# Moving three steps' query and key transposes from TensorE to the crossbar DMA in an attention-and-mixer kernel

## The chip, the core and the metric

The kernel runs on one core of a Trainium2 chip. The core has a matrix engine (TensorE; PE in the profile, with its weight loads as PEld), a vector engine (VectorE, DVE), a scalar engine (ScalarE, ACT), GpSimd (POOL), a queue processor that only issues work (SyncE, SP), and 16 DMA engines. Each engine runs its own list of instructions in order and waits on semaphores for the others. The metric is the device time of one execution in microseconds, lower being better; the number compared is the median of several executions.

## What is computed

An attention layer with squared ReLU in place of softmax feeds an MLP mixer. Sizes: batch 8, 12 heads, sequence 448, head size 64, so a model width of 768.

```python
scores = (q @ k.T) / sqrt(64)                   # per batch and head, 448 x 448
attn   = maximum(scores, 0)**2 / 448
x      = (attn @ v), heads side by side         # 8 x 448 x 768
u      = x + (maximum(x.T @ w_tok1, 0) @ w_tok2).T     # token mixing, 448 -> 256 -> 448
out    = u + maximum(u @ w_ch1, 0) @ w_ch2             # channel mixing, 768 -> 1536 -> 768
```

Matrix products take bf16 operands; inputs and output are float32.

## The kernel before, in words

**Steps.** The work is cut into 24 steps of four heads each (`ND`, three steps to a batch element). For step i the kernel needs queries and keys with the head dimension on the partitions, so the loaded tiles `q_raw` and `k_raw`, which have tokens on the partitions, must be transposed. Then seven score tiles (`scores`, L211) go through ScalarE's ReLU (L231) and VectorE's squaring (L238); `values` (L240) multiplies them with v into the two PSUM tiles `acc0` and `acc1`; `values_out` (L259) scales the result into `xT`.

**Mixer.** One step behind, `x_back` transposes `xT` back to tokens (by TensorE up to step 7, by DMA from step 8 on: `XDMA` = 8, L294), `token1`, `token1_main` and `token1_rest` (L339, L355) and `token2` (L380, L390) do the token mixing and write `uT_sb`. Units of channel mixing, `channel1` (L431) and `channel2` (L470, output addition L477), are put in a Python list, and `fill` hands them out between the pieces of the steps by a credit in nominal cost, so that TensorE always has something to do. The order of instructions is fixed when the program is built; nothing is reordered at run time.

**The residual.** The addition at L477 needs u with tokens on the partitions. `u_back` (L407) gets it by DMA transposes of `uT_sb` into `u_sb` (L413), two transfers per step of heads, issued on SP. Six of them, those of batch element 0, are issued at the end of loop pass i = 7, and `hold_back` (L418) makes them wait: GpSimd writes one element into each target after it has read `uT_sb` of that pass, so no transfer may start sooner. A second `hold_back`, in pass 8, stands ahead of the next six.

**Transposing q and k.** Up to step 11 `transposes` (L125) does it on TensorE: 56 small products into `acc0` and `acc1` (L140), then two copies by VectorE (L154). From step 12 on (`TDMA` = 12) VectorE first interleaves the two tiles into `qk_sb` (`interleave`, L192, one buffer), and one DMA transpose, issued on SP, writes `qkT_x` (`transposes_dma`, L198). `qk_of` (L204) picks the layout by the same constant. The DMA form is prepared two passes ahead, the TensorE form one pass ahead.

**Queues.** SP issues, in program order, all DMA transposes (L198, L294, L413) and the output transfers (L489). GpSimd issues the loads of q, k and v three steps ahead (`load_four`, L83), and of the weights. `out_sb` has three buffers, `raw` tiles have four of each name, and the two PSUM tiles tagged `bank` serve all channel products in turn.

The loop from L661 on is where the order is written out by hand. Pass i holds, in this order: two score tiles of step i, the values of step i-1, a third score tile, interleaving and fill, `x_back`, the residual's transfers, `transposes_dma`, the loads, squares, two score tiles, TensorE transposes of step i+1, squares, fill, first token product, two score tiles, squares, fill, second token product, `hold_back` and the six residual transfers (pass 7 only), squares, fill.

Of the kernel before, what the change touches and what calls it, by code (L numbers as in the profile page):

```python
# [16 lines left out]
def kernel(  # L17
# [19 lines left out]
    ND = B * H // 4  # L37
# [143 lines left out]
            else:  # L181
                nc.vector.tensor_copy(sb[:, :, 0], queries[:, :, :S])

    TDMA = 12
    qk_tiles = {}

    def interleave(i):

        t = attn.tile([128, 2, QC, 2, D], BF16, name="qk_sb", bufs=1)
        qk_tiles[i] = t  # L190
        for w in range(2):
            nc.vector.tensor_copy(  # L192
                t[:, w].rearrange("n c g d -> n g c d"), raws.pop((i, "qk"[w]))
            )

    def transposes_dma(i):
        sb = attn.tile([128, 2, QC, 128], BF16, tag="qkT", name="qkT_x", bufs=3)
        nc.sync.dma_start_transpose(  # L198
            out=sb.rearrange("n w c t -> n (w c) t"),
            in_=qk_tiles.pop(i).rearrange("n w c g d -> n (w c g d)"),  # L200
        )
        qkT[i] = sb

    def qk_of(i, h, r):  # L204
        sb = qkT[i]
        if i < TDMA:
            return sb[h, r, 0, :], [sb[h, r, 1, c * 64 : (c + 1) * 64] for c in range(QC)]
# [3 lines left out]
    def scores(i, c, alone=False):  # L211
        ps = ps_att.tile([128, 2, 512], FP32, tag="att", name="sc_ps")
        for r in range(2):
            for g in range(2):
                h = slice(64 * g, 64 * (g + 1))
                queries, keys = qk_of(i, h, r)
                nc.tensor.matmul(  # L217
                    ps[64 * r : 64 * (r + 1), g, :S],
                    lhsT=keys[c],
                    rhs=queries,  # L220
                    start=True,
                    stop=True,
                    skip_group_check=True,
                )
        at = attn.tile([128, 2, S], BF16, name="at", bufs=11)
        if alone:
            nc.vector.tensor_scalar(
                out=at, in0=ps[:, :, :S], scalar1=0.0, scalar2=None, op0=ALU.max
            )
        else:  # L230
            nc.scalar.activation(at, ps[:, :, :S], AF.Relu)  # L231
        squares.append(at)
        at2[i, c] = at

    def square(keep=0):
        while len(squares) > keep:
            at = squares.pop(0)
            nc.vector.tensor_tensor(out=at, in0=at, in1=at, op=ALU.mult)  # L238

    def values(i, cs):  # L240
        v_raw = raws[i, "v"]
        if i not in accs:
            accs[i] = [ps_acc.tile([128, 512], FP32, tag=f"acc{r}", name="acc_ps") for r in range(2)]
        ps = accs[i]
        for c in cs:
            at = at2.pop((i, c))
            for r in range(2):
                for g in range(2):
                    h = slice(64 * r, 64 * (r + 1))
                    nc.tensor.matmul(  # L250
                        ps[r][64 * g : 64 * (g + 1), :S],
                        lhsT=v_raw[h, g, c, :],
                        rhs=at[h, g, :],
                        start=(c == 0),
                        stop=(c == QC - 1),
                        skip_group_check=True,
                    )

    def values_out(i, split=False):  # L259
        b, d = divmod(i, DB)  # L260
        ps = accs.pop(i)
        for r in range(2):
            if split and r == 1:
                nc.scalar.activation(
                    xT[b % 2][:, 2 * d + r, :S], ps[r][:, :S], AF.Copy, scale=float(alpha2)
                )
                continue
            nc.vector.tensor_scalar(  # L268
                out=xT[b % 2][:, 2 * d + r, :S],
                in0=ps[r][:, :S],  # L270
                scalar1=float(alpha2),
                scalar2=None,
                op0=ALU.mult,
            )
        if i > 2 * DB - 1:
            for r in range(2):
                nc.vector.tensor_scalar(
                    out=xT[b % 2][:, 2 * d + r, S:],
                    in0=ps[r][:, S - 64 : S],
                    scalar1=float(alpha2),  # L280
                    scalar2=None,
                    op0=ALU.mult,
                )
# [119 lines left out]
    def chunks(b):  # L403
        half = NT // 2
        return range(half) if b % 2 == 0 else range(half, NT)
# [12 lines left out]
    def hold_back(b, src):  # L418

        u_tiles[b] = mix.tile([128, NP, NT - NT // 2, 128], BF16, name="u_sb", bufs=3)  # L420
        for p in range(NP):
            nc.gpsimd.tensor_copy(u_tiles[b][:1, p, 0, :1], src)

    def channel1(b, e):
        if b % 2 == 0 and e == 0 and b > 0:
            r2_tiles[b // 2] = mix.tile([128, EC, 2 * S], BF16, name="r2_sb")
        uT, r2 = uT_tiles[b // 2], r2_tiles[b // 2]
        off = (b % 2) * S
        ps = ps_mm.tile([128, 512], FP32, tag="bank", name="m1_ps")
        for g in range(CC):  # L430
            nc.tensor.matmul(  # L431
                ps[:, :S],
                lhsT=wc1[:, g, e * 128 : (e + 1) * 128],
                rhs=uT[:, g, off : off + S],
                start=(g == 0),
                stop=(g == CC - 1),
            )
        nc.scalar.activation(r2[:, e, off : off + S], ps[:, :S], AF.Relu)  # L438
# [87 lines left out]
    def channel_work(b):  # L526
        for e in range(2 if b == 0 else 0, EC):
            queue.append((C1, lambda e=e: channel1(b, e)))
        for t in chunks(b):
            for j in range(2):  # L530
                last = b == B - 1 and t == NT - 1 and j == 1
                unit = channel2_last if last else channel2
                args = (b, t) if last else (b, t, j)
                later.append((C2, lambda unit=unit, args=args: unit(*args)))
        if b > 0:
            queue.extend(later)
            later.clear()
# [91 lines left out]
    i = DB  # L629
# [31 lines left out]
    for i in range(DB + 1, ND + 2):  # L661
        slow = i <= 2 * DB
        back = i - 1 < ND
        if i == 2 * DB + 1:
            rate[0] = (EC * C1 + NT * C2) / DB
        if i < ND:
            scores(i, 0)
            scores(i, 1)
        if 0 <= i - 1 < ND:
            values(i - 1, range(QC))  # L670
            values_out(i - 1)
        if i < ND:
            scores(i, 2)
        if TDMA <= i + 2 < ND:
            interleave(i + 2)
        if i - 1 < XDMA:
            fill(1 / 3, least=1)
        if 0 <= i - 1 < ND:
            x_back(i - 1)
        since[0] = 0.0  # L680
        if i > 2 * DB + 1:
            if i == 2 * DB + 2:
                hold_back(1, x_tiles[i - 1][:1, 0, 0, :1])
            while u_later and u_later[0] < max(i - 1 - (i == 2 * DB + 2), 0):
                u_back(u_later.pop(0))
        if TDMA <= i + 2 < ND:
            transposes_dma(i + 2)
        if i + PRE < ND:
            if i - 1 >= XDMA:
                nc.gpsimd.tensor_copy(gate, x_tiles[i - 1][:1, 1, 3, 127:])  # L690
            load_four(i + PRE)
        if i == 5:
            load_wc2(1, 2)
            load_wt1_last()
        square()
        if i - 1 >= XDMA:
            fill(0.37, least=1)
        if i < ND:
            scores(i, 3)
            scores(i, 4)  # L700
        if i + 1 < min(ND, TDMA):
            transposes(i + 1)
        square()
        if slow:
            token1(i - 1)
            fill(1 / 3, least=1)
        else:
            fill(0.37, least=1, upto=4400 if back else 0)
            if back:
                token1_main(i - 1)  # L710
        if i < ND:
            if not slow:
                token1_rest(i - 1)
            scores(i, 5)
            scores(i, 6)
        elif back:
            token1_rest(i - 1)
        if not slow:
            square()
            fill(0.1, least=1)  # L720
        if back:
            token2(i - 1)
            if (i - 1) % DB == DB - 1:
                channel_work((i - 1) // DB)
        if i == 2 * DB + 1:
            hold_back(0, uT_tiles[1][:1, 0, :1])
            for _ in range(DB):
                u_back(u_later.pop(0))
        square()
        fill(1 / 3 if slow else 0.16, least=1)  # L730
    while queue:
        queue.pop(0)[1]()
# [30 lines left out]
```

## Time and profile before

| what | value |
|---|---|
| median of 10 runs | 371.26 us (370.96 to 373.02) |
| the profiled execution | 371.23 us |
| its span in the profile | 369.5 us |
| TensorE busy | 359.9 us, 97% of the span |
| VectorE / ScalarE / GpSimd busy | 207.3 / 210.3 / 98.4 us |
| DMA moved | 48.75 MB, mean 132 GB/s |
| TensorE clock granted | 0.999 |

The span begins with the first and ends with the last recorded instruction; the execution's own time is 1.7 us longer. A matrix engine that is busy 97% of the time is the first place to look, but a share is only an average: the view of the chain of work that ended last tells stage by stage whether it waited for anything. Loop pass 7 begins at about 69.5 us of the span, pass 8 at 84.4, pass 9 at 101.7, pass 10 at 116.8, pass 11 at 131.9.

### The profile page before, as it was taken

The numbers are of one execution on the slowest core, as the hardware profiler recorded it, in microseconds if no ns is written. First come the engines' busy times: TensorE is split into PE (matmuls) and PEld (weight loads), VectorE is DVE, ScalarE is ACT, GpSimd is POOL, SyncE is SP. The second block draws the span as 40 slices with busy tenths as digits, with TensorE's granted clock in tenths as the row PEclk, the third lists the DMA queues.
The fourth block names the chain that finished last, engine by engine and source line by source line (L and its number), as shares of the span: only waits on it lengthen the run. The fifth ranks groups of instructions, "written<-read, shape, count | busy, mean of one in ns | idle before, by whom it ended". The sixth has DMA issues, their size and how long they took to land.

```text
span 369.5 us, 8951 instructions
## 1 busy us (share of the span) xinstructions
PE 359.9 (97%) x3705; PEld 193.8 (52%) x3705; DVE 207.3 (56%) x414; ACT 210.3 (57%) x313; POOL 98.4 (27%) x185
## 2 busy tenths in 40 slices
PE   8889999999999999999999999999999999999995
PEld 3534555455555544555455545455445555555563
DVE  2986688756675774565654674575564674221031
ACT  3987888777245467735775457753875456402400
POOL 8957348112312404430421403412300000000000
PEclk9999999999999999999999999999999999999999
DMA  8999999952999899869768889859682624233023
GB/s 152 123 192 189 185 207 133 169 76 57 128 180 159 131 239 141 157 118 209 138 110 152 127 184 181 142 100 208 127 145 52 135 56 89 59 71 87 0 70 103
DMA packets 91449, 48.75 MB, mean 132 GB/s; under 512 B 65360, under 2 KB 87952, under 8 KB 91408
## 3 DMA queue, kind: packets, MB, share of 16 engines
q0 software_dynamic: 24496, 21.49, 41.5%
q1 hardware_dynamic: 66528, 26.26, 33.5%
q8 instruction: 29, 0.48, 0.5%
q10 hardware_dynamic: 384, 0.43, 0.4%
q14 instruction: 12, 0.10, 0.1%
HBM read 43.42 MB, written 11.01 MB: 147 GB/s over the span
## 4 chain that ended last, share of the span: by engine, by line
PE 88%; DVE 7%; ACT 1%; DMA 1%; issue 1%; POOL 0%; DVEq 0%; POOLq 0%; ACTq 0%
PE m_ps L470 29%; PE m_ps L431 28%; PE acc_ps L250 9%; PE sc_ps L217 9%; PE h_ps L380 4%; PE t_ps L339 3%; DVE at L238 3%; PE t_ps L321 1%; DVE uT_sb L390 1%; DMA q_raw<-in_q_dram 1%; PE t_ps L355 1%; ACT at L231 1%; PE qkT_ps L140 1%; DVE qkT L154 1%; PE x_ps L303 1%
## 5 line engine op out<-in xcount | busy, mean ns | idle before, releaser
L231 ACT ACTIVATE at<-sc_ps 128x896 bf16<-128x896 f32 x167 | 144.7, 924 | 49.4 <-PE sc_ps L217 45.0
L238 DVE TENSOR_TENSOR at<-at 128x896 bf16<-128x896 bf16 x168 | 98.1, 620 | 61.8 <-ACT at L231 61.7
L431 PE MATMUL m_ps<-uT_sb,wc 128*128 128x448 bf16 x564 | 115.7, 353 | 0.4 <-DVE out_sb L477 0.2
L470 PE MATMUL m_ps<-wc,r_sb 128*128 128x384 bf16 x660 | 113.2, 326 | 0.0
L470 PEld LDWEIGHTS <-r_sb 128*128 128x128 bf16 x660 | 62.7, 98 | 47.9 <-issue 7.5
L438 ACT ACTIVATE r_sb<-m_ps 128x448 bf16<-128x448 f32 x94 | 51.5, 548 | 53.4 <-PE m_ps L431 53.4
L431 PEld LDWEIGHTS <-wc 128*128 128x128 bf16 x564 | 52.3, 98 | 56.3 <-issue 11.6
L477 DVE TENSOR_TENSOR out_sb<-m_ps,u_sb 128x384 f32<-128x384 f32 x55 | 30.5, 554 | 46.8 <-PE m_ps L470 46.8
L250 PE MATMUL acc_ps<-at,v_raw 64*64 64x448 bf16 x672 | 40.7, 351 | 1.5 <-DVE x_sb L312 0.7
L268 DVE TENSOR_SCALAR xT<-acc_ps 128x448 bf16<-128x448 f32 x45 | 26.1, 619 | 27.6 <-PE acc_ps L250 27.6
L83 POOL DMA_DIRECT2D q_raw<-in_q_dram x48 | 29.0, 614 | 23.7 <-DMA wc<-in_moe_w_ch_dram 20.2
L690 POOL COPY gate<-x_sb 1x1 bf16<-1x1 bf16 x12 | 2.3, 192 | 122.3 <-DMA x_sb<-xT 122.3
L390 DVE TENSOR_TENSOR uT_sb<-h_ps,xT 128x448 bf16<-128x448 f32 x48 | 27.7, 616 | 9.4 <-PE h_ps L380 9.3
L83 POOL DMA_DIRECT2D v_raw<-in_v_dram x48 | 29.6, 643 | 6.9 <-DMA wc<-in_moe_w_ch_dram 5.5
L250 PEld LDWEIGHTS <-v_raw 64*64 64x64 bf16 x672 | 21.4, 106 | 15.7 <-issue 5.7
L365 ACT ACTIVATE r_sb<-t_ps 128x256 bf16<-128x256 f32 x36 | 11.9, 381 | 30.2 <-PE t_ps L355 30.2
L217 PE MATMUL sc_ps<-qkT 64*64 64x448 bf16 x336 | 27.5, 360 | 1.1 <-ACT at L231 1.0
L83 POOL DMA_DIRECT2D k_raw<-in_k_dram x46 | 28.1, 634 | 1.8 <-issue 1.7
L217 PE MATMUL sc_ps<-qkT_x 64*64 64x448 bf16 x336 | 25.7, 356 | 0.0
L380 PE MATMUL h_ps<-wt,r_sb 128*128 128x448 bf16 x96 | 22.3, 353 | 0.0
L217 PEld LDWEIGHTS <-qkT 64*64 64x64 bf16 x336 | 9.2, 105 | 13.0 <-issue 10.8
L339 PE MATMUL t_ps<-x_sb,wt 128*128 128x256 bf16 x108 | 14.7, 273 | 0.0
(62 smaller groups left out, 162.9 us busy)
## 6 DMA issues: line engine op xcount, KB each, us to landing
out_dram<-out_sb SPq DMA_DIRECT2D x54, 192.0 KB, 3.1
q_raw<-in_q_dram POOLq DMA_DIRECT2D x48, 112.0 KB, 4.6
v_raw<-in_v_dram POOLq DMA_DIRECT2D x48, 112.0 KB, 6.0
k_raw<-in_k_dram POOLq DMA_DIRECT2D x46, 112.0 KB, 6.1
wc<-in_moe_w_ch_dram POOLq DMA_DIRECT2D x4, 1152.0 KB, 12.5
u_sb<-uT_sb SPq DMA_TRANSPOSE x48, 2.5
x_sb<-xT SPq DMA_TRANSPOSE x16, 3.2
k_first<-in_k_dram SPq DMA_DIRECT2D x1, 224.0 KB, 3.5
```

The source lines that it names most:

```text
L83: eng.dma_start(out=dst[64 * r : 64 * (r + 1)].rearrange("p g c d -> p g (c d)"), in_=src[b, h0 : h0 + 2].rearrange("g (p c) d -> p g (c d ...
L217: nc.tensor.matmul(ps[64 * r : 64 * (r + 1), g, :S], lhsT=keys[c], rhs=queries, start=True, stop=True, skip_group_check=True,)
L231: nc.scalar.activation(at, ps[:, :, :S], AF.Relu)
L238: nc.vector.tensor_tensor(out=at, in0=at, in1=at, op=ALU.mult)
L250: nc.tensor.matmul(ps[r][64 * g : 64 * (g + 1), :S], lhsT=v_raw[h, g, c, :], rhs=at[h, g, :], start=(c == 0), stop=(c == QC - 1), skip_gro ...
L268: nc.vector.tensor_scalar(out=xT[b % 2][:, 2 * d + r, :S], in0=ps[r][:, :S], scalar1=float(alpha2), scalar2=None, op0=ALU.mult,)
L380: nc.tensor.matmul(parts[r][:, :S], lhsT=r1[:, j, r * 128 : (r + 1) * 128], rhs=wt2[:, j, :], start=(j == 0), stop=(j == JC - 1),)
L390: nc.vector.tensor_tensor(out=uT_tiles[b // 2][:, 2 * d + r, off : off + S].rearrange("n (c p) -> n c p", c=QC), in0=parts[r][:, :S].rearr ...
L431: nc.tensor.matmul(ps[:, :S], lhsT=wc1[:, g, e * 128 : (e + 1) * 128], rhs=uT[:, g, off : off + S], start=(g == 0), stop=(g == CC - 1),)
L438: nc.scalar.activation(r2[:, e, off : off + S], ps[:, :S], AF.Relu)
L470: nc.tensor.matmul(ps[:, :HN], lhsT=r2[:, e, t * 128 : (t + 1) * 128], rhs=wc2[:, e, cols], start=(e == 0), stop=(e == EC - 1),)
L477: nc.vector.tensor_tensor(out=o[:, cols].rearrange("n (g d) -> n g d", d=128), in0=ps[:, :HN].rearrange("n (g d) -> n g d", d=128), in1=u_ ...
```

## The change

`TDMA` goes from 12 to 9, so queries and keys of steps 9, 10 and 11 go by the crossbar too. Steps 9 and 11 are prepared at the loop's usual place, in passes 7 and 9. Step 10 would have been prepared in pass 8; it is prepared at the end of pass 7 instead, ahead of `hold_back` and the six residual transfers on the program's list. The last `square()` of a pass moves above these lines.

```diff
-    TDMA = 12
+    TDMA = 9
...
-        if TDMA <= i + 2 < ND:
+        crossed = (TDMA, *range(TDMA + 2, ND))
+        if i + 2 in crossed:
             interleave(i + 2)
...
-        if TDMA <= i + 2 < ND:
+        if i + 2 in crossed:
             transposes_dma(i + 2)
...
             token2(i - 1)
             if (i - 1) % DB == DB - 1:
                 channel_work((i - 1) // DB)
+        square()
+
+        if i == TDMA - 2:
+            interleave(TDMA + 1)
+            transposes_dma(TDMA + 1)
         if i == 2 * DB + 1:
             hold_back(0, uT_tiles[1][:1, 0, :1])
             for _ in range(DB):
                 u_back(u_later.pop(0))
-        square()
         fill(1 / 3 if slow else 0.16, least=1)
```

## The prediction

> **What bounds the kernel now.** I read the chain of work that ended last first, then its pieces in order of time around passes 7 to 10, then the timelines of SP and VectorE there, then the DMA issues one by one. The chain's shares:
>
> ```profile
> PE 88%; DVE 7%; ACT 1%; DMA 1%; issue 1%; POOL 0%; DVEq 0%; POOLq 0%; ACTq 0%
> ```
>
> TensorE carries 88% of it. In order of time (start, length, what), the stretch that the edit touches:
>
> ```profile
> 90.16 0.48 PE qkT_ps L140 x56
> 90.64 1.24 PE m_ps L431 x6
> ...
> 101.81 0.50 PE sc_ps L217 x8
> 102.31 1.32 PE acc_ps L250 x28
> ...
> 106.39 0.48 PE qkT_ps L140 x56
> ...
> 110.87 0.66 PE t_ps L339 x6
> ...
> 121.47 0.48 PE qkT_ps L140 x56
> ```
>
> From 75 us to 134 every piece is TensorE and the pieces touch: TensorE waits for nothing there. So a transposition taken away is time saved one for one, if nothing else becomes late. The question is what does, and how close it is now. SP's timeline (start, length):
>
> ```profile
> 84.82 16.83 SPq L413 DMA_TRANSPOSE u_sb<-uT_sb  x12
> 101.75 2.47 SPq L489 DMA_DIRECT2D out_dram<-out_sb  x4
> 105.16 1.23 SPq L294 DMA_TRANSPOSE x_sb<-xT  x1
> 106.44 6.14 SPq L413 DMA_TRANSPOSE u_sb<-uT_sb  x4
> ```
>
> SP is full from 84.82 to 104.2: twelve residual transfers at about 1.3 us each, then outputs that had been ready since 96.4. Whatever is put ahead of the twelve shifts them all. VectorE's timeline shows their first reader:
>
> ```profile
> 83.94 1.15 DVE L390 TENSOR_TENSOR uT_sb<-h_ps,xT 128x448 bf16<-128x448 f32 x2
> ...
> 94.04 0.55 DVE L477 TENSOR_TENSOR out_sb<-m_ps,u_sb 128x384 f32<-128x384 f32 x1
> 95.88 0.56 DVE L477 TENSOR_TENSOR out_sb<-m_ps,u_sb 128x384 f32<-128x384 f32 x1 [1.29 <-PE m_ps L470]
> ```
>
> The L477 at 94.04 reads columns 0 to 2 of the residual (transfers 1 to 3), the one at 95.88 columns 3 to 5 (transfers 4 to 6). Looked up one by one, the sixth, issued at 91.39, lands 4.0 us later at 95.4, **0.5 us before its use**; the seventh, issued at 93.38, takes 7.3 (the k load issued at 93.5 stands beside it; last figure, us from issue to landing):
>
> ```profile
> u_sb<-uT_sb SPq DMA_TRANSPOSE x1, 4.0
> ...
> k_raw<-in_k_dram POOLq DMA_DIRECT2D x1, 112.0 KB, 5.2
> u_sb<-uT_sb SPq DMA_TRANSPOSE x1, 7.3
> ```
>
> Before the loads of step 11 begin (issued by GpSimd from 92.33 to 95.9) a residual transfer lands 2.3 to 2.4 us after issue; issued among them, 7.3, 7.7 and 6.5.
>
> **Part by part.**
>
> *Removed: three sets of TensorE transposes* (steps 9, 10, 11, in passes 8, 9, 10). By the chain 0.48 us each, all on the path: 3 x 0.48 = **-1.44 us**. The unit rows (0.39 for q and 0.43 for k, overlapping) bound one between 0.43 and 0.82; the gap in the chain is what its successors would move up by, so I take 0.48.
>
> *VectorE.* Two L154 copies (615 ns each) go per step and two L192 copies (385 and 384 ns; the pair at 120.10 to 120.79) come, one or two passes earlier. Pass 7 gets two pairs. The first falls into the idle 1.6 us ahead of the `x_sb` copy at 74.50; k of step 9 was issued at 62.0 and 62.6 and took 11.5, so lands at 74.1, and the pair ends near 74.6: 0.1 us late, then hidden by VectorE's 3.65 us of idle before 82.58. Without that cover it would cost that 0.1. The second pair starts after the L390 at 83.94 (ends 85.09) and ends at 85.8, inside the 1.43 us idle before 86.51; q and k of step 10, issued 72.1 to 74.4, had landed by 78.3. The pair of step 11 in pass 9 takes 0.7 us of a VectorE that loses 1.2 there. All at zero.
>
> *The transfer of step 9*, issued in pass 7 near 73.7 while SP has nothing else until 84.82: read at 101, lands in 3.9 to 9.6 by the twelve `qkT_x` transfers. Zero. Buffers: `qk_sb` is free again by 84; `qkT` has three, and step 7's is read out by 81.4. Zero. The `square()` that moves finds nothing to do after pass 6.
>
> *The transfer of step 10*, **the costly part**. It makes SP wait for VectorE until 85.8 instead of 84.82 and then takes 1.54 us of issue (median row) plus a 0.1 us gap; transfer 1 goes from 84.82 to 87.4, a shift of 2.6 us. Behind the wait on SP stand all twelve residual transfers, four outputs and `x_back` of step 8. The sixth goes from 91.39 to 94.0, into the loads, whose time doesn't move (GpSimd waits for the `x_sb` copy at 89.70, ahead of the removed transposes). Bounds of its landing: 94.0 + 2.4 = 96.4 (as if undisturbed) to 94.0 + 7.7 = 101.7. The nearest rows are the transfers issued at 93.38 (landed 100.7) and 94.70 (102.4); since those have four blocks and this three, I take **101.0**.
>
> What waits then: L477 (needed at 95.4), and behind it on VectorE, in order, two squares (1.15), the next L477 (0.55) and two L390 (1.15), the last of which free `acc0` and `acc1` for the values at 102.31. With the first L477 itself: 0.55 + 1.15 + 0.55 + 1.15 = 3.4, so values start at 101.0 + 3.4 = 104.4 in place of 102.31 - 0.48 = 101.8: **TensorE stalls 2.6 us**. By the bounds it is 0 to 3.3; it begins when the landing passes 98.4. Transfers 1 to 3 aren't late: issued by 90.1, behind a `qkT_x` that lands by about 91.8 (the median row, 6.0 us), needed at 93.5.
>
> The Trainium skill, page "Advanced Engine Details and Errata", section "X-Bar Transpose (TRN2)", says that transposing DMAs are as fast as regular ones, 350 to 400 GB/s. By it the sixth residual transfer (0.1 MB) would move in 0.3 us and the sum be a gain; the rows above, 2.4 us alone and over 7 among loads, speak against using it.
>
> *`x_back` of step 8.* SP comes free at 104.2 + 2.6 = 106.8, not before; its data would be ready at 105.16 - 0.48 = 104.7 without the stall, at 107.3 with it. With the stall it costs nothing more; without, see rival 1. *The transfer of step 11* in pass 9 delays two outputs' issue by 1.5 to 3.5 us (rows L198); `out_sb` has 3.2 us there (landed 121.7, next written 124.90) and the stall shifts the writer too. `x_back` of step 9 may land behind it: it had 2.4 us (123.4 against 125.8). Cost 0 to 1.0; I take 0, the other transfers of this kind having cost none.
>
> *Sum*, against the profiled execution (371.23, of which 369.5 span): 371.23 - 1.44 + 2.6 = **372.4 us**. The profiled execution stands 0.03 under the median of the runs, which is nothing.
>
> **Rivals.**
>
> 1. *The residual comes in time, but `x_back` of step 8 is late* (landing before 98.4). SP issues it at 106.8; the one row of this place took 4.4, the others 3.1: landing 109.9 to 111.2, needed at 110.71 - 0.96 = 109.75. Stall 0.2 to 1.5, total 370.0 to 371.3. For it: SP is full either way. Against: the seventh transfer's 7.3.
> 2. *Nothing becomes late*: 371.23 - 1.44 = 369.8, **faster**. One mechanism decides: whether crossbar transfers keep their pace beside the loads. If the sixth lands less than 4.4 us after issue (by 98.4) and SP makes up 2 us, by the first six following each other faster than 1.3 us, the gain is whole. For it: the DMA share between 84 and 92 is only 0.26 to 0.38, so there is room for 0.46 MB more. Against: SP's issue, not the DMA engines, sets the pace there.
> 3. *The change does less than it says*: TensorE's saved 0.48 goes to another engine each pass, VectorE or ScalarE, total near 371.2. For it: VectorE and ScalarE set the pace around 64 to 69 us. Against: from 75 on TensorE's pieces touch.
>
> **How the numbers follow.** A measurement of this kernel can tell about 0.2% (0.74 us), so "same" is 370.5 to 372.0. The forecast's case, the late residual, has 0.62: its own range is 370.9 (landing at 99.5: 99.5 + 3.4 - 101.8 = 1.1 of stall) to 373.7 (landing at 101.7, 3.3 of stall, with 0.6 more from `x_back` of step 9), 0.52 of it slower and 0.10 same. Rival 1 has 0.22 (0.10 faster, 0.12 same), rival 2 0.10 (faster), rival 3 0.06 (0.04 same, 0.02 faster). Together: faster 0.22, same 0.26, slower 0.52. The range reaches from rival 1's lower end to the forecast's upper one: 370.0 to 373.7.
>
> **What would show it.** Right: in pass 8 a wait of the second L477 for DMA `u_sb`, 4 to 6 us long, then a gap in TensorE before L250 in pass 9; the residual's sixth landing over 6 us after issue; 56 fewer L140 products in each of passes 8 to 10; SP's first residual transfer near 87.4. Wrong: the second L477 still released by TensorE, or TensorE's gap ahead of L339 in pass 9 (rival 1). The prediction fails most easily at the sixth transfer's landing: each microsecond there is one in the result.

## The result and the profile after

The changed kernel takes **375.46 us** (median of 8 runs, 375.16 to 376.55) against 371.22 for the kernel before (29 runs): a ratio of 1.0112, 95% interval 1.0101 to 1.0124. It is 4.2 us slower. The direction was forecast, the size was not: 372.4 was expected and the range ended at 373.7. The profiled execution took 375.57, its span 373.8. Three more executions of the changed kernel, which the median leaves out, are on record with 372.45, 373.09 and 375.52 us.

The chain of work that ended last, shares by engine, of the changed kernel:

```profile
PE 81%; DMA 6%; DVE 6%; POOL 4%; issue 1%; ACT 1%; SPq 0%; DVEq 0%; ACTq 0%; POOLq 0%
```

DMA, 1% before, has 6%, and TensorE's share is 7 points lower. Where that sits is in the chain's pieces in order of time (start, length, what):

```profile
94.18 7.08 DMA u_sb<-uT_sb
...
102.09 3.47 PE m_ps L470 x12
...
115.49 10.21 DMA qkT_x<-qk_sb
...
128.12 0.48 DVE out_sb L477
128.64 2.11 PE m_ps L470 x12
```

Two transfers now set the end: one of the residual in pass 8, and the queries and keys of step 11 in pass 9. The first was predicted. SP's and VectorE's timelines of the same kernel show it (start, length, engine and line, and in brackets the idle time before and what ended it):

```profile
85.52 1.54 SPq L198 DMA_TRANSPOSE qkT_x<-qk_sb  x1
87.11 16.69 SPq L413 DMA_TRANSPOSE u_sb<-uT_sb  x12
```

```profile
93.19 0.56 DVE L477 TENSOR_TENSOR out_sb<-m_ps,u_sb 128x384 f32<-128x384 f32 x1 [0.39 <-PE m_ps L470]
101.47 0.56 DVE L477 TENSOR_TENSOR out_sb<-m_ps,u_sb 128x384 f32<-128x384 f32 x1 [7.73 <-DMA u_sb<-uT_sb]
...
123.10 0.34 DVE L277 TENSOR_SCALAR xT<-acc_ps 128x64 bf16<-128x64 f32 x2
125.82 0.40 DVE L192 COPY qk_sb<-q_raw 128x896 bf16<-128x896 bf16 x1 [2.38 <-DMA qkT_x<-qk_sb]
```

The twelve residual transfers start at 87.11 in place of 84.82, 2.6 us later against TensorE's own time (pass 8 begins 0.26 us earlier in this execution). The sixth is issued at 94.18 and lands 7.1 us later, and the second L477 waits 7.73 us for it. The last line is new: in pass 10 VectorE waits 2.38 us to interleave step 12, because the single `qk_sb` buffer is still being read by step 11's transfer. On TensorE both waits appear one instruction later, through the `bank` tiles that L477 frees:

```profile
98.21 0.92 PE L380 MATMUL h_ps<-wt,r_sb 128*128 128x448 bf16 x4
102.09 3.47 PE L470 MATMUL m_ps<-wc,r_sb 128*128 128x384 bf16 x12 [2.96 <-DVE out_sb L477]
...
124.67 2.12 PE L470 MATMUL m_ps<-wc,r_sb 128*128 128x384 bf16 x12
128.64 2.11 PE L470 MATMUL m_ps<-wc,r_sb 128*128 128x384 bf16 x12 [1.84 <-DVE out_sb L477]
```

And a third thing: the twelve products at 102.09 take 3.47 us where twelve of the same kind take 2.11 at 128.64. The view by stages (columns: stretch, its length, busy time of PE, PEld, DVE, ACT, POOL, granted TensorE clock, DMA share, GB/s) gives the reason:

```profile
101.00:102.00 1.00, 0.00 (x0) 0.00 (x0) 0.53 (x2) 0.00 (x0) 0.00 (x0) 0.73 1.68 143
102.00:103.00 1.00, 0.91 (x4) 0.40 (x3) 1.00 (x3) 0.00 (x0) 0.00 (x0) 0.50 1.42 167
103.00:104.00 1.00, 1.00 (x5) 0.48 (x4) 1.00 (x3) 0.00 (x0) 0.00 (x0) 0.50 1.32 262
104.00:105.00 1.00, 1.00 (x5) 0.50 (x4) 0.63 (x2) 0.00 (x0) 0.00 (x0) 0.56 2.05 179
```

While TensorE stands idle its granted clock falls to half, and it works on at half from 102.09 until near 104.9 (0.56 as the mean of the last stretch).

Each of the eleven executions of the changed kernel also has its mean granted clock on record. By these rows the clock was at half for some 3.4 us, from 101.5 to 104.9. That takes 1.7 of 373.8 us from the mean, 0.0046, so a mean of 0.995 (the profiled execution) means one such stretch. Of the eight timed executions seven have 0.994 or 0.995 (375.20 to 376.55 us) and one 0.999 (375.16). Of the three others, 375.52 has 0.994, and 372.45 and 373.09 have 0.999.

**The balance.** I measure the time from TensorE's first score products of pass 8 to those of pass 11, which takes in everything that the edit touches. These are the first and the last of them, before and then after (TensorE's timelines):

```profile
84.42 0.57 PE L217 MATMUL sc_ps<-qkT 64*64 64x448 bf16 x8
...
131.92 0.57 PE L217 MATMUL sc_ps<-qkT 64*64 64x448 bf16 x8
```

```profile
84.16 0.57 PE L217 MATMUL sc_ps<-qkT 64*64 64x448 bf16 x8
...
136.71 0.57 PE L217 MATMUL sc_ps<-qkT_x 64*64 64x448 bf16 x8
```

It was 47.50 us before and is 52.55 after, 5.05 more. From start to start on TensorE, which leaves out how the ends of products are modelled, the parts are these:

- the three sets of transposes: -1.44;
- the first gap: +3.12 (L470 starts 3.88 us after L380 in place of 0.76; 2.96 of it is marked as idle);
- the half clock: +1.35 (3.39 us from these twelve products to the next scores in place of 2.04);
- the second gap: +2.01 (5.92 us for the twenty-four products of pass 10 in place of 3.91; 1.84 of it is marked as idle).

That makes 5.04. The other passes and the ends give 0.7 us back in this pair of executions, as executions of one kernel differ.

### The profile page after: what moved, and what is told of

Same layout as the page of the kernel before. It is cut to its first block, busy times and chain, and to the rows that moved or that the text cites. A ratio compares the mean times of both kernels' runs of the same rounds, so it can differ in the third digit from the quotient of the medians.

```text
span 373.8 us, 8626 instructions
## 1 busy us (share of the span) xinstructions
PE 360.0 (96%) x3537; PEld 192.1 (51%) x3537; DVE 206.1 (55%) x414; ACT 210.3 (56%) x313; POOL 100.6 (27%) x185
## 4 chain that ended last, share of the span: by engine, by line
PE 81%; DMA 6%; DVE 6%; POOL 4%; issue 1%; ACT 1%; SPq 0%; DVEq 0%; ACTq 0%; POOLq 0%
PE m_ps L431 28%; PE m_ps L470 25%; PE acc_ps L250 8%; PE sc_ps L217 8%; PE h_ps L380 4%; PE t_ps L339 3%; DMA qkT_x<-qk_sb 3%; DMA u_sb<-uT_sb 2%; DVE at L238 2%; PE t_ps L321 1%; DVE uT_sb L390 1%; PE t_ps L355 1%; DMA k_raw<-in_k_dram 1%; POOL q_raw L83 1%; POOL wt L96 1%
## 5 line engine op out<-in xcount | busy, mean ns | idle before, releaser
L470 PE MATMUL m_ps<-wc,r_sb 128*128 128x384 bf16 x660 | 114.7, 329 | 4.8 <-DVE out_sb L477 4.8
L470 PEld LDWEIGHTS <-r_sb 128*128 128x128 bf16 x660 | 63.1, 98 | 54.7 <-issue 15.1
L477 DVE TENSOR_TENSOR out_sb<-m_ps,u_sb 128x384 f32<-128x384 f32 x55 | 30.5, 554 | 54.1 <-PE m_ps L470 46.4
L250 PE MATMUL acc_ps<-at,v_raw 64*64 64x448 bf16 x672 | 40.7, 351 | 1.6 <-DVE x_sb L312 0.8
L691 POOL COPY gate<-x_sb 1x1 bf16<-1x1 bf16 x12 | 3.4, 286 | 126.6 <-DMA x_sb<-xT 126.6
L390 DVE TENSOR_TENSOR uT_sb<-h_ps,xT 128x448 bf16<-128x448 f32 x48 | 27.7, 616 | 9.4 <-PE h_ps L380 9.3
L217 PE MATMUL sc_ps<-qkT_x 64*64 64x448 bf16 x420 | 31.8, 356 | 0.0
L250 PEld LDWEIGHTS <-v_raw 64*64 64x64 bf16 x672 | 21.4, 106 | 15.7 <-issue 5.8
L380 PE MATMUL h_ps<-wt,r_sb 128*128 128x448 bf16 x96 | 22.3, 353 | 0.0
L217 PE MATMUL sc_ps<-qkT 64*64 64x448 bf16 x252 | 21.4, 361 | 0.9 <-ACT at L231 0.8
L217 PEld LDWEIGHTS <-qkT_x 64*64 64x64 bf16 x420 | 10.3, 105 | 11.1 <-issue 9.8
L339 PE MATMUL t_ps<-x_sb,wt 128*128 128x256 bf16 x108 | 14.7, 273 | 0.0
```

Of the source, the lines that this page charges most:

```text
L217: nc.tensor.matmul(ps[64 * r : 64 * (r + 1), g, :S], lhsT=keys[c], rhs=queries, start=True, stop=True, skip_group_check=True,)
L250: nc.tensor.matmul(ps[r][64 * g : 64 * (g + 1), :S], lhsT=v_raw[h, g, c, :], rhs=at[h, g, :], start=(c == 0), stop=(c == QC - 1), skip_gro ...
L380: nc.tensor.matmul(parts[r][:, :S], lhsT=r1[:, j, r * 128 : (r + 1) * 128], rhs=wt2[:, j, :], start=(j == 0), stop=(j == JC - 1),)
L390: nc.vector.tensor_tensor(out=uT_tiles[b // 2][:, 2 * d + r, off : off + S].rearrange("n (c p) -> n c p", c=QC), in0=parts[r][:, :S].rearr ...
L470: nc.tensor.matmul(ps[:, :HN], lhsT=r2[:, e, t * 128 : (t + 1) * 128], rhs=wc2[:, e, cols], start=(e == 0), stop=(e == EC - 1),)
L477: nc.vector.tensor_tensor(out=o[:, cols].rearrange("n (g d) -> n g d", d=128), in0=ps[:, :HN].rearrange("n (g d) -> n g d", d=128), in1=u_ ...
```

## The experiments

Two theories went into the first runs. **Theory A**: the order on SP makes the residual late, the stall costs clock, and the one `qk_sb` buffer makes the second stall; the three add up. **Rival B**: the crossbar's traffic as such, beside the loads, slows every transpose, wherever it is put. Rivals C, D and E belong to single runs. "Stage" below is the time from pass 8 to pass 11 in the profiled execution, 47.50 before and 52.55 after; TensorE's sum is 47.50 less 0.48 for each step moved plus the waits found; a wait costs some 0.2 us more than the idle time that the timeline marks, as the balance shows. The last column counts the runs whose mean granted clock was 0.995 or less; of 81 executions of the kernel before that have a clock on record, 2 are of that kind, its slowest (373.23 and 373.24).

| run | steps by crossbar | median us (range) | ratio to before, 95% | stage us | clock 0.995 or less |
|---|---|---|---|---|---|
| after | 9, 10 early, 11 | 375.46 (375.16 to 376.55) | 1.0101 to 1.0124 | 52.55 | 7 of 8 |
| only 9 | 9 | 370.61 (369.84 to 371.20) | 0.9968 to 0.9990 | 47.02 | 0 of 12 |
| only 10 | 10 early | 373.92 (372.39 to 375.34) | 1.0048 to 1.0098 | 50.33 | 4 of 6 |
| only 11 | 11 | 372.61 (371.59 to 375.02) | 1.0029 to 1.0070 | 49.06 | 3 of 12 |
| 10 at its usual place | 9, 10, 11 | 374.27 (372.92 to 376.95) | 1.0056 to 1.0119 | 50.26 | 3 of 6 |
| 10 behind six residuals | 9, 10, 11 | 375.20 (373.81 to 375.47) | 1.0069 to 1.0116 | 50.60 | 4 of 5 |
| no crossing, residual later | none | 376.11 (373.54 to 377.59) | 1.0087 to 1.0148 | 51.87 | 5 of 6 |
| after, two `qk_sb` | 9, 10 early, 11 | 373.60 (372.36 to 374.35) | 1.0031 to 1.0072 | 49.31 | 3 of 8 |
| after, idle products | 9, 10 early, 11 | 374.71 (373.71 to 377.12) | 1.0067 to 1.0120 | 50.91 | 1 of 6 |
| 9 and 11, two `qk_sb` | 9, 11 | 371.06 (369.87 to 375.87) | 0.9967 to 1.0014 | 48.33 | 2 of 12 |
| outputs behind `x_back` | 9, 10, 11 | 373.29 (371.31 to 375.11) | 1.0022 to 1.0065 | 49.89 | 4 of 12 |
| all behind `x_back` | 9, 10, 11 | 371.83 (371.07 to 374.47) | 1.0002 to 1.0040 | 46.07 | 4 of 12 |
| 9, 10 behind `x_back` | 9, 10 | 370.68 (370.25 to 371.24) | 0.9971 to 0.9992 | 46.55 | 0 of 10 |

### One step at a time

A set of steps (`XBAR`) replaces the limit, and only one of 9, 10 and 11 is in it.

```diff
-    TDMA = 9
+    XBAR = {9, *range(12, ND)}        # or 10, or 11
...
-        if i < TDMA:
+        if i not in XBAR:
...
-        if i + 1 < min(ND, TDMA):
+        if i + 1 < ND and i + 1 not in XBAR:
```

> Of the three steps only step 9 goes by the crossbar (pass 7, usual place); 10 and 11 stay on TensorE. Theory A: its transfer has SP and the DMA engines to itself, 371.2 - 0.48 = 370.7 us. Rival B: the crossbar costs wherever it is put, 371.2 us or more.

> Only step 10 goes by the crossbar, at the end of pass 7 ahead of the residual; 9 and 11 stay on TensorE. Theory A: the whole first stall, 2.96 + 1.52, and no other: 371.2 - 0.48 + 4.5 = 375.2 us (somewhat less, since step 9's transposes on TensorE give the residual 0.5 us). Rival B: the loss is shared by the three transfers, 372.5 us.

> Only step 11 goes by the crossbar, in pass 9 at the usual place; 9 and 10 stay on TensorE. Theory A: the wait of step 12's interleave for qk_sb, 2.0 us of TensorE, less 0.48: 371.2 + 1.5 = 372.7 us. Rival B: 372.5 us too, but with the wait elsewhere (L477 or L339).

Step 9 alone gains 0.46 us (370.61 against 371.07 for the kernel before, timed beside it), stage -0.48: its transfer costs nothing. Step 11 alone loses 1.5, as expected, and by the expected wait (VectorE's timeline of that run):

```profile
122.60 0.39 DVE L192 COPY qk_sb<-q_raw 128x896 bf16<-128x896 bf16 x1 [2.42 <-DMA qkT_x<-qk_sb]
```

Step 10 alone has the whole first gap, 2.98 us, without any other crossing, but 373.92 us where 375.2 was expected. TensorE's timeline of that run tells the difference:

```profile
98.78 0.92 PE L380 MATMUL h_ps<-wt,r_sb 128*128 128x448 bf16 x4
102.67 2.11 PE L470 MATMUL m_ps<-wc,r_sb 128*128 128x384 bf16 x12 [2.98 <-DVE out_sb L477]
```

The same gap as after the change, and the next twelve products at full speed: in this execution the clock didn't fall. It did in four of the six runs (373.70 to 375.34), and not in the two others (372.39 and 373.56). So the loss of clock isn't a fixed companion of the gap. Rival B falls: the loss isn't shared out among the three steps, it is nothing, 2.9 and 1.5. Added up these make 3.9, where the three together cost 4.2.

### Late without any traffic: the residual held back, no step moved

In the kernel before, `hold_back` reads `xT` of pass 8 in place of `uT` of pass 7.

```diff
-        if i == 2 * DB + 1:
-            hold_back(0, uT_tiles[1][:1, 0, :1])
-            for _ in range(DB):
-                u_back(u_later.pop(0))
...
             values_out(i - 1)
+        if i == 2 * DB + 2:
+            hold_back(0, xT[0][:1, 2, :1])
+            for _ in range(DB):
+                u_back(u_later.pop(0))
```

> The kernel before with no crossing added; only the hold of the six residual transfers reads xT of step 7 instead of uT of step 6, so that the first is issued near 87.4 us in place of 84.8, as in the changed kernel, with no qkT_x transfer ahead of it. Theory A (being issued 2.6 us later, among the loads, is what makes them late): L477 waits over 5 us for u_sb, TensorE loses 3.0 us and, if the clock falls, 1.5 more: 374 to 375.7 us. Rival D (the bytes of the step 10 transfer ahead of them delay them): 371.2 us, no wait at L477.

It takes 376.11 us, with L477 waiting 7.24 us:

```profile
87.19 16.41 SPq L413 DMA_TRANSPOSE u_sb<-uT_sb  x12
```

```profile
101.62 0.56 DVE L477 TENSOR_TENSOR out_sb<-m_ps,u_sb 128x384 f32<-128x384 f32 x1 [7.24 <-DMA u_sb<-uT_sb]
```

This is the clearest run of the study. The start on SP (87.19) and the landing are those of the changed kernel, with not one byte of `qkT_x` ahead of them. Being issued later is the cause (the first transfer by 2.4 us, the sixth at 94.39 in place of 91.39); the transfer that caused the lateness only had to occupy SP. Rival D falls. That it is the loads which slow a transfer issued then is read from the landings beside them; no run here moved the loads.

### Step 10's transfer at two other places

```diff
         if i == TDMA - 2:
             interleave(TDMA + 1)
-            transposes_dma(TDMA + 1)
         if i == 2 * DB + 1:
             hold_back(0, uT_tiles[1][:1, 0, :1])
             for _ in range(DB):
                 u_back(u_later.pop(0))
+        if i == TDMA - 2:
+            transposes_dma(TDMA + 1)
```

> Only the place of step 10's transfer on SP changes: behind the six residual transfers of pass 7 in place of ahead of them. Theory A (order on SP, cold clock, one qk_sb buffer): the sixth residual transfer is issued near 91.4 again and lands by 95.5, the 7.7 us wait of L477, TensorE's gap of 2.96 us and the 1.5 us at half clock go; the wait of VectorE for qkT_x in pass 10 stays (2.0 us of TensorE). 375.5 - 4.5 = 371.0 us, up to 372 if x_back of step 8 comes late. Rival B (it is the volume of crossbar traffic beside the loads that slows all transposes, the order is indifferent): 375 us and again a wait of over 5 us at the second L477.

The residual is in time again, as theory A says, but the run missed its number: 375.2 where 371 to 372 was expected (374.35 in the profiled execution). What came in place of the first stall is a wait that I had priced at 1 us at most:

```profile
111.70 0.81 PE L339 MATMUL t_ps<-x_sb,wt 128*128 128x256 bf16 x6 [1.77 <-DMA x_sb<-xT]
```

SP issues the last of twelve residual transfers and four outputs until 107.75, and only then `x_back` of step 8, whose data were ready near 104.6; it lands 3.9 us later. This is the prediction's first rival. The wait for `qk_sb` stays (2.44 us on TensorE). The stage's sum is 47.50 - 1.44 + 1.77 + 2.44 = 50.3, measured 50.60. The median of the five runs is 0.85 over the profiled execution. That one kept the full clock and the four others didn't, but one of these is the fastest of all (373.81), so the rest isn't explained.

> Steps 9 to 11 by the crossbar, each at the loop's usual place: step 10 is interleaved and issued in pass 8, behind all twelve residual transfers. Theory A: no wait at L477, but SP is full until x_back of step 8, which comes 1.6 us later than SP would be free now and finds TensorE waiting at L339 in pass 9 for about 1 us; the wait of pass 10 for qk_sb stays (2.0): 371.2 - 1.44 + 3.0 = 372.8 us. Rival B: 375 us.

With step 10 at the loop's usual place the result, 374.27, is between the two expectations, and the mechanism is another than I wrote. TensorE's timeline of that run:

```profile
109.93 2.11 PE L470 MATMUL m_ps<-wc,r_sb 128*128 128x384 bf16 x12 [2.04 <-DVE out_sb L477]
...
126.54 2.11 PE L470 MATMUL m_ps<-wc,r_sb 128*128 128x384 bf16 x12 [1.84 <-DVE out_sb L477]
```

Both gaps come from VectorE's waits for `qk_sb` (2.58 us in pass 9, step 11 behind step 10, and 2.37 in pass 10, step 12 behind step 11). So the early place of step 10 in the change does save one such wait, and pays for it with the residual's.

### A second `qk_sb` buffer

A second tile of its own doesn't fit: with it 6.3 KB per partition are left where `out_sb`'s pool needs 9, so the two kernels planned that way, one of them with step 10 behind the six residual transfers, have no time. But `k_first` is read out in the first step and has the right size; odd steps use it.

```diff
-        t = attn.tile([128, 2, QC, 2, D], BF16, name="qk_sb", bufs=1)
+        if i % 2:
+            t = k_first.bitcast(BF16).rearrange("n w c (g d) -> n w c g d", g=2)
+        else:
+            t = attn.tile([128, 2, QC, 2, D], BF16, name="qk_sb", bufs=1)
```

> The changed kernel with a second qk_sb buffer, laid over k_first, which is read out after the first step; odd steps use it. Theory A: VectorE's wait for qkT_x in pass 10 goes and with it 2.0 us: 373.5 us. Rival E (pass 10 only changes what is late, since x_back of step 9 stands behind the same traffic): 375 us with a wait at L339.

373.60 us, 1.9 less than after the change: the second gap is gone, and the whole remaining one is the first (2.92 us, here too without loss of clock in the profiled execution: stage 47.50 - 1.44 + 2.92 = 49.0, measured 49.31). Part of the 1.9 may be clock: three of these eight runs lost it, seven of eight after the change. Runs that lost it compare as 374.22 with 375.48 (medians), 1.3 us. Rival E falls: no wait at L339 (L342 in this kernel).

> Steps 9 and 11 by the crossbar, step 10 on TensorE, two qk_sb buffers (the second over k_first). Theory A: neither stall is left: 371.2 - 0.96 = 370.2 us. Rival E: step 11's transfer in pass 9 still makes x_back of step 9 or the outputs late: 371.5 us or more.

Inconclusive in time: 371.06 with runs from 369.87 to 375.87, the two slowest being those that lost clock. The profiled execution (372.12) shows TensorE waiting 0.87 and 0.58 us for `x_sb` in passes 9 and 10.

### Keeping TensorE busy in the gap

```diff
+        if i == TDMA - 1:
+            idle_ps = ps_att.tile([128, 512], FP32, tag="att", name="idle_ps")
+            for _ in range(8):
+                nc.tensor.matmul(idle_ps, lhsT=warm[:, :128], rhs=warm, start=True, stop=True)
         fill(1 / 3 if slow else 0.16, least=1)
```

> The changed kernel with eight added matrix products on constant data, into a score tile that nobody reads, put on TensorE in pass 8 after the second token product, where TensorE stands idle for 2.96 us. Theory A (half a clock's loss follows from the idle time): the next 12 products of L470 take 2.1 us in place of 3.5 and the time falls by 1.5 to 374.0 us. Rival C (they are slow because their weights or the PSUM are busy with late transfers, not by the clock): 375.5 us, and L470 again 3.5 us.

The gap shrinks to 1.29 us, the clock stays at 1.00 throughout and the next products take 2.11, so rival C falls. Pass 8 is 1.30 us shorter than in the changed kernel. The stage is 1.64 shorter, because the second gap is smaller in this execution too (1.33 us idle), which the idle products don't explain, and pass 9 is 0.17 longer. The profiled execution itself took 375.47, its pass 8 beginning 1.7 us later than in the changed kernel. The median, 374.71, is only 0.75 under the changed kernel's, and the runs scatter over 3.4 us.

That half the clock is what slows the products is shown by the granted clock beside them. That the idle gap is what brings it down is supported by the runs' own clocks: one run of six lost clock with the gap filled, seven of eight without, and none of the 22 of the two versions that stall least (step 9 alone, and 9 and 10 behind `x_back`). A gap doesn't always bring it: two profiled executions above had one of 2.98 and 2.92 us and kept the clock.

### Can the gain be had?

Three runs follow what the others showed: let nothing that is needed soon stand behind a `qkT_x` transfer. The first puts step 10 behind six residual transfers, takes two `qk_sb` buffers and issues the four outputs behind `x_back` of step 8. The other two issue step 10's (and 11's) transfer directly behind `x_back`, one pass before its use. In the first, on top of the diffs above, in `channel2` and in the loop:

```diff
+                held.append(issue) if b == 0 and t < 2 else issue()   # issue: the output transfer
...
             x_back(i - 1)
+        while i == XDMA + 1 and held:
+            held.pop(0)()
```

In the other two:

```diff
             x_back(i - 1)
+        if i + 1 in behind:               # {10, 11}, or {10}
+            transposes_dma(i + 1)
...
-        if i + 2 in crossed:
+        if i + 2 in crossed - behind:
             transposes_dma(i + 2)
```

> Steps 9 to 11 by the crossbar, step 10's transfer behind the first six residual transfers, two qk_sb buffers, and the four output transfers that stood ahead of x_back of step 8 on SP issued behind it. Theory A: all three waits go and the three removed transposes are whole: 371.2 - 1.44 = 369.8 us. Rival E: SP is 0.6 us short ahead of x_back of step 8 and 1 us ahead of that of step 9, and TensorE waits at L339: 371 us.

> Steps 9 to 11 by the crossbar with two qk_sb buffers; the transfers of steps 10 and 11 are issued directly behind x_back of steps 8 and 9, in passes 9 and 10, one pass ahead of their use. Theory A: nothing that is needed soon stands behind a qkT_x transfer, so 371.2 - 1.44 = 369.8 us, if the transfers land within 10 us; step 11's, issued near 121.7, would be 0.5 to 1 us late for pass 11: then 370.5 us. Rival E (every added crossbar transfer in passes 8 to 10 comes back as a wait): 371.2 us or more.

> Steps 9 and 10 only, step 10's transfer directly behind x_back of step 8; step 11 stays on TensorE; two qk_sb buffers. Theory A: 371.2 - 0.96 = 370.2 us. Rival E: outputs and x_back of step 9 come late behind it and TensorE waits at L339: 371.2 us or more.

The first loses nothing in passes 8 and 9, then 2.03 us at L339 in pass 10 (SP spends 5.06 us on step 11's transfer ahead of outputs and `x_back` of step 9), and again the clock falls behind the gap. With all three behind `x_back`, passes 8 to 10 take 46.07 us, 1.43 less than before: **the whole predicted gain of 1.44 is there**. It is given back in pass 11 (1.96 us longer than before), where `x_back` of step 10 now stands behind two crossings and six outputs:

```profile
130.20 4.33 SPq L492 DMA_DIRECT2D out_dram<-out_sb  x6
134.64 1.32 SPq L297 DMA_TRANSPOSE x_sb<-xT  x1
```

```profile
134.64 5.29 DMA x_sb<-xT
139.93 0.05 issue
139.98 0.83 PE t_ps L342 x6
```

(The first fence is SP's timeline, the second the chain in order of time; L492, L297 and L342 are L489, L294 and L339 of the kernel before. TensorE waits 1.79 us for that landing.) SP issues this `x_back` only 0.3 us later in its pass than before the change, 3.79 us after the pass begins in place of 3.50. The loss is in the landing: 5.29 us in place of 3.25, with the outputs issued just ahead still landing until 139.03. Steps 9 and 10 alone keep 0.95 us until pass 11 and give back 0.73 there: 370.68, the same as step 9 alone at 370.61. These two are the versions that beat both kernels, by 0.2%.

## Why the prediction was wrong, point by point

- **The removed transposes**: right. 0.48 us each; -0.48, -0.95 and -1.43 in the stage with one, two and three steps where nothing else is late.
- **The residual's lateness**: right in the transfer and the reader, near in size, wrong in where TensorE stops. Predicted: sixth transfer issued at 94.0, landing at 101.0, a wait of 4 to 6 us at the second L477, then TensorE idle before L250 in pass 9 for 2.6 us, through the L390 that free `acc0` and `acc1`. Measured: 94.18, 101.25, a wait of 7.73 (VectorE came to it earlier, having nothing else), and TensorE idle 2.96 us already before L470 in pass 8, through the `bank` tile that the late L477 itself frees; L250 had no wait of its own. That both ways give nearly the same stall is luck. The price was put on SP's time, the wait and the issue, and not on the bytes of step 10's transfer; the run without any crossing bears that out. One reading was too neat: of the transfers issued before the loads only the first four landed in 2.3 to 2.4 us, the fifth and sixth took 3.8 and 4.0.
- **"The transfer of step 11 ... Cost 0 to 1.0; I take 0, the other transfers of this kind having cost none"**: this is the first of two steps that failed. I had checked `qk_sb` for steps 9 and 10 ("free again by 84") and the three `qkT` buffers, but not who writes `qk_sb` next after step 11: step 12's interleave in pass 10, with VectorE's squares and additions queued behind it. The upper end of the `qkT_x` row that I quoted, 3.9 to 9.6 us, was enough to see the danger, its median of 6.0 was not: issued at 115.49, the transfer lands at 125.70, and VectorE is ready at 123.4. It cost 2.0 us of TensorE here, and as much in the run with step 11 alone (1.5 after the 0.48 saved).
- **The stall's price**: the second step that failed, "TensorE stalls 2.6 us" taken as the whole price of the gap. In the changed kernel the clock fell to half behind it, another 1.35 us. No row of the trace before could show this (mean granted clock 0.999), and two profiled executions had such a gap without it (2.98 and 2.92 us); as an unknown it belonged in the range and was not there.
- With the two missing terms the forecast would have been 372.4 + 2.0 + 1.35 = 375.8 us; the profiled execution took 375.57. That this is so near is partly chance: the first gap cost 0.5 us more than the 2.6 forecast, and 0.7 came back outside the stage. Nor are the two terms there in every execution: two of the eleven on record, with the clock at 0.999, took 372.45 and 373.09 us, inside the forecast's range, and no profile shows what they waited for.
- **Rival 1** (`x_back` of step 8 late behind SP) was real: it decides as soon as the residual is put first, 1.77 us. **Rival 2** asked whether crossbar transfers keep their pace beside the loads; they don't (7.1 us). **Rival 3** shows nowhere.

The Trainium skill, page "TensorE: Matmul & The Clock Gate", section "Part 1: The HAM clock gate (the "warmup" mystery)", describes the halving: the clock goes from full to half after an idle window of about 3.4 us, and the window runs freely. The runs agree on the half, and 3.4 us shows in them as the length of the half clock: by the granted clock it lasted from 101.47 to 104.88 here, from 103.29 to 106.70 in the run with the residual held back, and from 127.04 to 130.46 in the run with the outputs behind `x_back`. They don't agree that a gap must reach 3.4 us: 2.96, 2.58 and 2.03 us were enough in these three, and in the changed kernel the clock was down 2.3 us after the gap began. That the window runs freely would let gaps of like length bring it or not; this fits the runs and isn't shown by them.

## What to carry to other kernels

A transfer that moves to a queue has three prices beside its own landing: what stands behind it on the issuing queue, the buffer that it holds until it lands, and who on an in-order engine waits for that buffer. Before calling a single-buffered staging tile free, find its next writer and compare the slowest landing of that kind, not the median, with the writer's time. And where a transfer lands half a microsecond before its use, a shift on its queue is the whole price: it may fall among the loads and take three times as long.

## What the runs showed that I had not expected

- A residual transpose issued at 91.39 landed in 4.0 us; issued at 94.18 it took 7.1. It is the moment, not the bytes ahead of it, that matters: 7.24 us of wait with no added transfer at all.
- Issuing one `qkT_x` transpose can hold SP for much longer than its usual 1.54 us: 3.48 us for step 9's in the run with step 10 at its usual place, with SP otherwise idle, and 5.06 for step 11's in the run with the outputs behind `x_back`, both in stretches where loads are in flight. Whether that is the issue itself or a wait inside it, the timeline doesn't tell.
- TensorE's clock can fall after the work has resumed. In the run with the residual held back the gap ended at 102.23; the clock was still full until 103.29 and half until 106.70:

```profile
102.00:103.00 1.00, 0.77 (x5) 0.48 (x5) 1.00 (x3) 0.00 (x0) 0.00 (x0) 1.00 1.13 226
...
104.00:105.00 1.00, 1.00 (x4) 0.29 (x2) 0.77 (x2) 0.00 (x0) 0.00 (x0) 0.50 0.40 84
```

- Kernels with such a gap scatter by 1.4 to 6 us from run to run, and the clock goes with it: in nine of the eleven kernels with a gap, every run with a mean clock of 0.995 or less is slower than every run with more. The medians of the two kinds lie 1.4 to 2.6 us apart where there are two runs or more of each, and 4.2 in the kernel with steps 9 and 11. A longer gap would lengthen a run and make the loss likelier at once, so how much of that is the clock itself isn't shown.
